# The first block's convolution branch of a fused adaLN, S4 convolution and SwiGLU kernel: row additions on GpSimd and high and low parts in place of fp32 products

## The chip, the cores and the metric

The kernel runs on one core of one Trainium2 chip. A core has five engines that run their own instruction streams: TensorE (PE, matrix products; its weight loads are listed apart as PEld), VectorE (DVE), ScalarE (ACT), GpSimd (POOL) and SyncE (SP, which here only issues DMAs). They hand work to each other by semaphores. Operands lie in SBUF, an on-chip memory of 128 partitions; TensorE writes its sums to PSUM, which VectorE and ScalarE read.

The metric is the time of one execution on the device in microseconds (us), as the median of several runs.

## The reference

`x` is 2048 rows of 448 channels. Six vectors come from a condition `c`; a layer norm scaled and shifted by two of them feeds a long convolution (S4), whose result is added to `x` through a gate; a second such norm feeds a SwiGLU with 1792 hidden channels, added through another gate.

```python
mod = (silu(c) @ w_mod).reshape(c.shape[0], 6, 1, -1)
sa, ca, ga, sb, cb, gb = (mod[:, i] for i in range(6))
h = layernorm(x) * (1 + ca) + sa
x = x + ga * A_ref(h, ...)            # the convolution along the rows
h = layernorm(x) * (1 + cb) + sb
x = x + gb * ((silu(h @ w_gate) * (h @ w_up)) @ w_down)

# A_ref, per channel d:
K[d, l] = real(sum_n C[d, n] * exp(dt[d] * A[d, n] * l) * dt[d] * B[d, n])
y = causal convolution of h with K along l (by FFT) + h * Dskip
```

## The kernel before

**Tiles and blocks.** The 2048 rows are 16 tiles of 128 rows, taken in six blocks (`BLOCKS = [2, 2, 3, 3, 3, 3]`). For each block `ffn` runs the SwiGLU over its tiles, in 14 groups of 128 hidden channels ("column groups", index `f`). `gate_up(f)` makes both projections of group `f` with 22 products into two PSUM banks; `down(f - 1)` stands behind it and adds three products a tile into the banks `DN[q]`. Between them ScalarE makes the silu `p` (L744), VectorE the gated product (L757), ScalarE its high part `phi` (L760) and VectorE its low part `plo` (L761).

**High and low parts.** A product in full fp32 costs TensorE several passes. The kernel splits an operand in a high part of a shorter type (fp32r) and the low rest, and makes three fast products: high by high, high by low, low by high. The weights are split too, and this happens only in block 0 (`fresh`), while they arrive: for each column group ScalarE casts the high parts (L123, L115) and VectorE subtracts the low ones, L125 and L127 for the gate and up weights `gu`, L117 for `wdl` of the down weights. So block 0 has all this work beside that of every block.

**The convolution as running sums.** A test on the decay (`flag`) sets two branches; these inputs take the one for small decay, `small_path`. There the convolution kernel is a straight line in `l`, so the convolution is two cumulative sums along the rows: products of gated parts `v0 = h * gm0` and `v1 = h * g0` with a triangular matrix of ones, `tri`. What the rows of earlier tiles add is carried in two rows of `run` (`run0` and `run1`): each tile leaves its sum in partition 127, a DMA on ScalarE's queue brings it to partition 0, and there it enters the next tile's sum.

**Stages.** While block `b` runs its SwiGLU, the convolution branch of block `b + 1`'s tiles runs beside it in small stages: `s0` makes `h`; `s1` the two gated parts (L908); `s2` adds the running rows to row 0 of the gated parts (L913, L914) and splits `v0` in `vh` (ScalarE, L921) and `vl` (VectorE, L922); `s3` multiplies `h` by `gd` (L927); `s4` makes three products (L933 to L935: `tri` with `vh`, `v1`, `vl`, in this order) and adds `h` to `x`; `s5` makes the next running rows (L957 to L959) and adds the sums to `x`. In block 0 another stage, `s4f`, stands for `s2` to `s4`: it leaves row 0 as it is, multiplies `v0` in full fp32 (L946), and adds the running rows by two fp32 products of one row (L947, L948). After the stages come the statistics of the second norm, the normalised tile `xn` (L193 on VectorE, L194 and L195 on ScalarE) and its transposes (L206), from which ScalarE takes the high part `hhi` and VectorE the low part `hlo`.

**What sets the order.** Each engine runs its instructions in the order in which the program issues them. The table `TIMES` gives it: for each block when the first norm's statistics are taken, its root, a list of half-steps for the stages and the second statistics of each tile, the second root, and the half-steps of `xn`. Half-step `h` means: in column group `h // 2`, right behind `gate_up` where `h` is even, behind `down` where it is odd. In `gate_up(f)` of block 0 the splits of weight group `f + 2` stand between the silu, product, `phi` and `plo` of group `f`. The opening, from the first load to the first product of block 0, follows a list written by hand, `PLAN`, with one word a step; `first_rows` and `gate_0` follow it at the start of block 0's branch.

**PSUM.** Eight banks: four turn round under `bank()`, three are `DN[0]` to `DN[2]`, one is `CV`.

Of the kernel before, what the change touches and what calls it, by code (L numbers as in the profile page):

```python
# [43 lines left out]
m1 k1 cpc gd h11 hd0 ck v01 sq0 o10 v10 w0 cbw o12 v11 w01 o01 o02 hd1 o13 o14 xh1 gc0 sa st0 fs sp gq r0 n10 spc x1 xn0 gc1 st1 sbt tr0  # L44
qtb sbc r1 fl n11 l1 gbk hi00 xn1 w02 tr1 hi01 lo00 hi1 lo01 lo1 d00 d01 w1 w11 gb w12"""
# [11 lines left out]
def tile_kernel(ctx, tc, x, a_re, a_im, b_re, b_im, c_re, c_im, log_dt,  # L57
# [54 lines left out]
    def split_d(j, part=None):  # L112
        hi, lo = wp[j]
        if not part:
            sc.copy(hi, wdn[j])  # L115
        if part != 0:
            ve.tensor_tensor(lo, wdn[j], f32(hi), op=OP.subtract)  # L117
# [16 lines left out]
    run0, run1 = run[:, 0, :], run[:, 1, :]  # L134
    ca1 = const.tile([128, D], F32)
# [133 lines left out]
    with tc.tile_pool(name="pre", bufs=1) as pre:  # L269
# [99 lines left out]
        def turned_to(ps, t):  # L369

            for k in range(4):
# [38 lines left out]
        def to_channels(q):  # L410
            pk[q] = bank()
            turned_to(pk[q], h2[q])
# [7 lines left out]
        def high(q, ks=range(4)):  # L420
            for k in ks:
                c_ = slice(q * 128, (q + 1) * 128)
                sc.activation(hhi[:, k, c_], pk[q][:, k * 128:(k + 1) * 128], AF.Identity, bias=sbc[:, k:k + 1])

        def low(q, ks=range(4)):
            for k in ks:
                c_ = slice(q * 128, (q + 1) * 128)
                ve.scalar_tensor_tensor(hlo[:, k, c_], pk[q][:, k * 128:(k + 1) * 128], sbc[:, k:k + 1], f32(hhi[:, k, c_]),
# [8 lines left out]
        def flag_sum():  # L437
            pe.matmul(psm["d"][0:1, 460:462], ones, sz, start=True, stop=True)

        def flag_of():  # L440
            zm = pre.tile([1, 1], F32)
            ve.tensor_reduce(zm, psm["d"][0:1, 460:462], axis=AX.X, op=OP.add)
# [28 lines left out]
            "qtb": copy(gb, lambda: psm["gq"][:, 0:D]), "gb": copy(gb, lambda: psm["gq"][:, 0:D]),  # L471
# [15 lines left out]
            **{f"xn{q}": (lambda q: lambda: sc.activation(h2[q], h2[q], AF.Copy, scale=n2.of[q][1]))(q) for q in range(2)},  # L487
            **{f"tr{q}": do(to_channels, q) for q in range(2)}, "hi1": do(high, 1),
# [6 lines left out]
            **{f"d0{z}": do(split_d, 0, z) for z in range(2)},  # L495
# [197 lines left out]
    def first_rows():  # L693

        e = slice(96, 128)
        sc.copy(run1[e], CV[e, 0:D])
# [374 lines left out]
```

## Time and profile before

| | us |
|---|---|
| median of 3 runs | 485.05 (484.31 to 485.37) |
| the profiled execution | 485.06 |
| its span from the first instruction to the last | 483.0 |
| TensorE busy | 471.6 |
| VectorE busy | 285.1 |
| ScalarE busy | 155.4 |
| GpSimd busy | 59.8 |

The mean clock that the throttle granted to TensorE was 0.999 of full speed, so no time goes to a lowered clock. Times below are microseconds from the start of the span. A line of the timeline reads: start, duration, engine, source line, operation, result and operands with their shapes, count of like instructions in a row, and in brackets how long the engine had stood idle before it and what it had waited for. A line of a group of instructions reads: source line, engine, operation, operands, count, then busy time in all, mean nanoseconds of one, idle time before them and what ended most of it. In such lines the buffers' numbers are left out, and names are those of the program: `bank`, `dn` and `cv` are PSUM banks, `raw` is a buffer that several things share in turn.

### The profile page before, as it was taken

Reading aid. Unit: us, or ns where it says so; the run is one execution under the profiler, and the core shown is the slowest. Engines: PE = TensorE matmul, PEld = TensorE weight load, DVE = VectorE, ACT = ScalarE, POOL = GpSimd, SP = SyncE. Lnnn points to the kernel's source line nnn. Section 1 sums busy time; section 2 is a strip of 40 time slices with the busy share of each in tenths; the row PEclk is TensorE's granted clock in tenths of the full one; section 3 lists DMA queues with packets and bytes.
Section 4 is the critical chain, followed back from the end, with each engine's and each line's share of the span. In section 5 each row is a group of like instructions: output and inputs, shape, how many; then the busy total and the mean of one; then the engine's idle time right before and its main releaser. Section 6 shows DMA issues by size and latency. Waiting matters only on the chain.

```text
span 483.0 us, 7024 instructions
## 1 busy us (share of the span) xinstructions
PE 471.6 (98%) x2743; PEld 444.9 (92%) x2743; DVE 285.1 (59%) x550; ACT 155.4 (32%) x336; POOL 59.8 (12%) x82
## 2 busy tenths in 40 slices
PE   6999999999999999999999999999999999999995
PEld 4668988999999999999999999999999999999995
DVE  4879998768876546573644757375475544221225
ACT  5876545522234222332312323331222232112111
POOL 1220000000000040310022221002241000000000
PEclk9999999999999999999999999999999999999999
DMA  8965563020001200111200011130001112000001
GB/s 307 405 225 165 194 188 103 0 96 2 1 2 39 58 1 0 45 38 51 92 25 0 2 44 46 43 115 0 2 2 44 45 43 77 22 1 0 1 1 62
DMA packets 18778, 31.24 MB, mean 65 GB/s; under 512 B 2608, under 2 KB 13488, under 8 KB 18736
## 3 DMA queue, kind: packets, MB, share of 16 engines
q1 hardware_dynamic: 18000, 30.52, 18.8%
q8 instruction: 23, 0.38, 0.3%
q10 hardware_dynamic: 736, 0.19, 0.2%
q14 instruction: 19, 0.16, 0.1%
HBM read 24.61 MB, written 6.03 MB: 63 GB/s over the span
## 4 chain that ended last, share of the span: by engine, by line
PE 92%; DMA 3%; DVE 2%; ACT 1%; issue 0%; POOL 0%; SPq 0%; ACTq 0%; DVEq 0%
PE bank L729 59%; PE dn L773 28%; DMA wm<-in_w_mod_groups_dram 2%; DMA x<-in_A_u_dram 1%; PE bank L238 1%; PE dn L449 1%; PE bank L934 1%; PE cv L933 1%; PE cv L935 0%; PE bank L947 0%; DVE x L812 0%; PE bank L206 0%; PE cv L946 0%; PE cv L948 0%; ACT raw L195 0%
## 5 line engine op out<-in xcount | busy, mean ns | idle before, releaser
L729 PE MATMUL bank<-hhi,gu 128*128 128x384 f32 (+1 forms) x1169 | 211.3, 320 | 0.0
L729 PEld LDWEIGHTS bank<-hhi,gu 128*128 128x128 f32 x1169 | 191.2, 188 | 3.1 <-issue 0.7
L729 PE MATMUL bank<-hlo,gu 128*128 128x384 f32 (+1 forms) x668 | 131.8, 319 | 0.0
L757 DVE TENSOR_TENSOR bank<-raw,bank 128x384 f32<-128x384 f32 (+1 forms) x69 | 36.9, 534 | 125.0 <-PE bank L729 121.6
L729 PEld LDWEIGHTS bank<-hlo,gu 128*128 128x128 f32 x668 | 110.2, 188 | 0.0
L760 ACT CAST phi<-bank 128x384 fp32r<-128x384 f32 (+1 forms) x83 | 36.9, 444 | 141.6 <-DVE bank L757 141.6
L744 ACT ACTIVATE raw<-bank 128x384 f32<-128x384 f32 (+1 forms) x70 | 32.9, 470 | 123.0 <-PE bank L729 114.9
L761 DVE TENSOR_TENSOR plo<-bank,phi 128x384 fp32r<-128x384 f32 (+1 forms) x83 | 42.5, 512 | 37.1 <-ACT phi L760 37.1
L773 PE MATMUL dn<-wdh,phi 128*128 128x448 f32 x218 | 58.3, 368 | 0.6 <-DVE run L698 0.4
L773 PE MATMUL dn<-wdh,plo 128*128 128x448 f32 x218 | 57.7, 366 | 0.0
L773 PE MATMUL dn<-wdl,phi 128*128 128x448 f32 x218 | 57.6, 365 | 0.0
L773 PEld LDWEIGHTS dn<-wdl,phi 128*128 128x128 f32 x218 | 41.0, 188 | 3.4
L773 PEld LDWEIGHTS dn<-wdh,plo 128*128 128x128 f32 x218 | 40.9, 188 | 3.3
L773 PEld LDWEIGHTS dn<-wdh,phi 128*128 128x128 f32 x218 | 38.9, 188 | 2.9 <-DVE run L698 0.7
L167 POOL TENSOR_SCALAR rsb<-mvb 128x1 f32<-128x1 f32 (+2 forms) x13 | 4.6, 354 | 171.9 <-DVE mvb L151 171.9
L167 POOL TENSOR_SCALAR rsa<-mva 128x3 f32<-128x3 f32 (+1 forms) x6 | 2.4, 396 | 116.1 <-DVE mva L151 116.1
L123 ACT CAST gu<-raw 128x1024 fp32r<-128x1024 f32 x14 | 14.6, 1046 | 0.0
L125 DVE TENSOR_TENSOR gu<-raw,gu 128x768 fp32r<-128x768 f32 x14 | 13.3, 953 | 0.1
L922 DVE TENSOR_TENSOR vl<-m,vh 128x448 fp32r<-128x448 f32 x12 | 9.1, 757 | 6.7 <-ACT vh L921 6.1
L908 POOL TENSOR_TENSOR m<-m,gm 128x448 f32<-128x448 f32 x9 | 10.4, 1154 | 21.4 <-DVE m L184 17.5
L194 ACT ACTIVATE raw<-raw,rsb 128x64 f32<-128x64 f32 x14 | 4.8, 346 | 21.0 <-DVE raw L193 11.9
L927 POOL TENSOR_TENSOR m<-m,gd 128x448 f32<-128x448 f32 x9 | 11.6, 1284 | 0.0
(232 smaller groups left out, 411.0 us busy)
## 6 DMA issues: line engine op xcount, KB each, us to landing
raw<-in_B_w_gate_up_dram SPq DMA_DIRECT2D x14, 512.0 KB, 3.9
rawd<-in_B_w_down_dram SPq DMA_DIRECT2D x16, 224.0 KB, 4.1
x<-in_A_u_dram SPq DMA_DIRECT2D x12, 224.0 KB, 3.3
out_dram<-x SPq DMA_DIRECT2D x11, 224.0 KB, 2.0
xd<-raw SPq DMA_DIRECT2D x9, 256.0 KB, 2.0
raw<-xd SPq DMA_DIRECT2D x36, 64.0 KB, 2.0
wm<-in_w_mod_groups_dram SPq DMA_DIRECT2D x5, 448.0 KB, 8.2
wm<-in_w_mod_groups_dram SPq DMA_DIRECT2D x5, 336.0 KB, 8.2
```

The lines of the kernel that those rows point to most:

```text
L123: sc.copy(wgu[j][:, :, 0:4, :], w)
L125: en.tensor_tensor(lo, w[:, :, 0:3, :], f32(hi), op=OP.subtract)
L167: po.tensor_scalar(rs[:, 0:n], self.mv[:, 0:n, 1], EPS, None, op0=OP.add)
L729: pe.matmul(ps[s][:, 0:n], w[:, s, a], (hlo if lo else hhi)[:, k, 0:n], start=first and q == 0, stop=end and q == len(ka) - 1)
L744: sc.activation(p[:, 0:n], ps[0][:, 0:n], AF.Silu)
L757: ve.tensor_tensor(ps[1][:, 0:n], p[:, 0:n], ps[1][:, 0:n], op=OP.mult)
L760: sc.copy(hi[:, 0:n], ps[1][:, 0:n])
L761: ve.tensor_tensor(lo[:, 0:n], ps[1][:, 0:n], f32(hi[:, 0:n]), op=OP.subtract)
L773: pe.matmul(dn[q][:, 0:D], u[:, cs], v, start=f == 0 and z == 0, stop=f == (NF - 3 if last else NF - 1) and z == 2)
L908: (ve if on_v else po).tensor_tensor(v, h, g, op=OP.mult)
L922: ve.tensor_tensor(vl, v0, f32(vh), op=OP.subtract)
L927: (ve if on_v else po).tensor_tensor(h, h, gd, op=OP.mult)
```

## The change

Line numbers behind the change are some 3 higher than before for the same code (`gate_up`'s L757 becomes L760, the row additions' L913 and L914 become L916 and L917, the gated parts' L908 becomes L911).

- **Block 0's branch.** `s4f` goes. The stages of block 0 are now `s0`, `s1`, `rows_p`, `s3`, `split`, `s4`, `s5`: the gated parts, both additions of running rows and the product with `gd` are GpSimd's, `split` makes `vh` and `vl`, and `s4` makes its three products, as in the other blocks. Block 0's row of `TIMES` has eight half-steps a tile instead of five, and the first norm's root stands at half-step 3 instead of 5.
- **The opening.** The three copies of `first_rows` become steps of `PLAN` (`fr1`, `fr0`, `fx`), ahead of the branch. The second tile's transposes go to two banks (a `bank()` for channels 0 to 255, `DN[2]` for the rest), its normalisation is shared (256 columns on ScalarE, 192 on VectorE), the copy of `gb` is VectorE's, the cast of the first high part of `w_down` comes earlier on ScalarE, and its low part is GpSimd's. The flag's sum goes to `CV`. In column group 0 the gate takes a `bank()` instead of `DN[2]`.
- **Block 1.** The half-steps of its three normalised tiles go from 23, 24, 24 to 23, 23, 23.

```diff
 TIMES = (
-    ((1, 1), 5, ((5, 10, 15, 15, 15), (9, 9, 18, 19, 19)), 19, (22, 23)),
-    ((2, 3, 3), 3, (...), 23, (23, 24, 24)),
+    ((1, 1), 3, ((5, 6, 8, 9, 11, 12, 13, 13), (9, 10, 15, 12, 17, 18, 19, 19)), 19, (22, 23)),
+    ((2, 3, 3), 3, (...), 23, (23, 23, 23)),
...
+    end = slice(96, 128)
...
         def flag_sum():
-            pe.matmul(psm["d"][0:1, 460:462], ones, sz, start=True, stop=True)
+            pe.matmul(CV[0:1, 460:462], ones, sz, start=True, stop=True)
...
-            "gb": copy(gb, lambda: psm["gq"][:, 0:D]),
+            "gb": lambda: ve.tensor_copy(gb, psm["gq"][:, 0:D]),
...
+            "xn1": lambda: sc.activation(h2[1][:, 0:256], h2[1][:, 0:256], AF.Copy, scale=n2.of[1][1]),
+            "xn1b": lambda: ve.tensor_scalar(h2[1][:, 256:D], h2[1][:, 256:D], n2.of[1][1], None, op0=OP.mult),
+            "fr1": copy(run1[end], CV[end, 0:D]), "fr0": add(run0[end], run1[end], DN[1][end, 0:D]),
+            "fx": copy(xs[0], DN[0][:, 0:D]),
+            "tr0": do(to_channels, 0), "tr1": do(to_channels, 1, (0, 1)), "tr1b": do(to_channels, 1, (2, 3)),
...
-            **{f"d0{z}": do(split_d, 0, z) for z in range(2)},
+            "d00": do(split_d, 0, 0), "d01": do(split_d, 0, 1, po),
...
     def first_rows():
-        e = slice(96, 128)
-        sc.copy(run1[e], CV[e, 0:D])
-        sc.copy(xs[0], DN[0][:, 0:D])
-        ve.tensor_tensor(run0[e], run1[e], DN[1][e, 0:D], op=OP.add)
         sc.dma_start(run[0:1], run[127:128])
...
-                ps = [DN[2] if fresh and f == 0 else bank(), bank()]
+                ps = [bank(), bank()]
...
+        def rows(i, en=ve):
             h, v0, v1 = vs[i]
+            en.tensor_tensor(v0[0:1], v0[0:1], run0[0:1], op=OP.add)
+            en.tensor_tensor(v1[0:1], f32(v1[0:1]), run1[0:1], op=OP.add)
+
+        def rows_p(i):
+            rows(i, po)
...
+        def split(i):
             h, v0, v1 = vs[i]
             vh = work.tile([128, D], F32R, name="vh")
             vl = work.tile([128, D], F32R, name="vl")
...
-        def s4f(i):
-            h, v0, v1 = vs[i]
-            o = CV[:, 0:D]
-            s = bank()[:, 0:D]
-            pe.matmul(s, tri, v1, start=True, stop=False)
-            pe.matmul(o, f32(tri), v0, start=True, stop=False)
-            pe.matmul(s, f32(tri[0:1, :]), run1[0:1], start=False, stop=True)
-            pe.matmul(o, f32(tri[0:1, :]), run0[0:1], start=False, stop=True)
-            s3(i, True)
-            ve.tensor_tensor(xs[i], h, xs[i], op=OP.add)
-            vs[i] = o, s
...
-        return lambda b: ((s0, v(s1), s4f, s5), (s0, v(s1), v(s2), v(s3), s4, s5),
-                          (s0, s1, v(s2), s3, s4, s5))[min(b, 2)]
+        return lambda b: ((s0, s1, rows_p, s3, split, s4, s5), (s0, v(s1), s2, v(s3), s4, s5),
+                          (s0, s1, s2, s3, s4, s5))[min(b, 2)]
```

The order of instructions shows three places. The first is GpSimd in block 0. Before, it stands still between the roots of the first norm (`rsa`) and of the second (`rsb`):

```order
L167 TENSOR_SCALAR rsa_613<-mva_512 128x2
L168 TENSOR_TENSOR rsa_613<-rsa_613,mhalf_107 128x2
L167 TENSOR_SCALAR rsb_984<-mvb_873 128x2
L168 TENSOR_TENSOR rsb_984<-rsb_984,mhalf_107 128x2
L167 TENSOR_SCALAR rsa_1268<-mva_1252 128x3
```

Now the two tiles' five instructions each stand there (`m5` holds two tiles' `h` and two tiles' `v0`; `run` holds the running rows):

```order
L169 TENSOR_TENSOR rsa_568<-rsa_568,mhalf_107 128x2
L911 TENSOR_TENSOR m5_79<-m5_79,gm0_91 128x448
L911 TENSOR_TENSOR v1_661<-m5_79,g0_90 128x448
L916 TENSOR_TENSOR m5_79<-m5_79,run_87 1x448
L917 TENSOR_TENSOR v1_661<-v1_661,run_87 1x448
L936 TENSOR_TENSOR m5_79<-m5_79,gd_94 128x448
L911 TENSOR_TENSOR m5_79<-m5_79,gm0_91 128x448
L911 TENSOR_TENSOR v1_763<-m5_79,g0_90 128x448
L936 TENSOR_TENSOR m5_79<-m5_79,gd_94 128x448
L916 TENSOR_TENSOR m5_79<-m5_79,run_87 1x448
L917 TENSOR_TENSOR v1_763<-v1_763,run_87 1x448
L168 TENSOR_SCALAR rsb_996<-mvb_834 128x2
```

So the second tile's row additions, which need the running rows that the first tile's `s5` leaves, stand behind its product with `gd`, and the second root stands behind all ten.

The second place is VectorE from the last steps of the opening to column group 0 (`gu` are weight groups, `hlo` the low part of the normalised tiles, L757 and L761 product and `plo` of a column group). Before:

```order
L127 TENSOR_TENSOR gu0_146<-raw_80,gu0_146 64x2x128
L428 SCALAR_TENSOR_TENSOR hlo_93<-bank_392,sbc_95,hhi_92 128x128 x4
L428 SCALAR_TENSOR_TENSOR hlo_93<-bank_414,sbc_95,hhi_92 128x128 x4
L117 TENSOR_TENSOR wdl0_151<-rawd0_81,wdh0_150 128x448
L125 TENSOR_TENSOR gu1_148<-raw_80,gu1_148 128x2x384
L127 TENSOR_TENSOR gu1_148<-raw_80,gu1_148 64x2x128
L503 TENSOR_LOAD flag_96
L1002 COMPARE_AND_BRANCH
L757 TENSOR_TENSOR bank_472<-p_469,bank_472 128x256
L125 TENSOR_TENSOR gu2_159<-raw_80,gu2_159 128x2x384
L761 TENSOR_TENSOR plo_471<-bank_472,phi_470 128x256
L127 TENSOR_TENSOR gu2_159<-raw_80,gu2_159 64x2x128
```

And now:

```order
L492 TENSOR_SCALAR h2_1_250<-h2_1_250,rsb_401 128x192
L474 COPY gb_76<-bank_370 128x448
L127 TENSOR_TENSOR gu0_146<-raw_80,gu0_146 64x2x128
L431 SCALAR_TENSOR_TENSOR hlo_93<-bank_393,sbc_95,hhi_92 128x128 x4
L431 SCALAR_TENSOR_TENSOR hlo_93<-bank_415,sbc_95,hhi_92 128x128 x2
L431 SCALAR_TENSOR_TENSOR hlo_93<-dn2_70,sbc_95,hhi_92 128x128 x2
L451 TENSOR_TENSOR run_87<-run_87,dn1_69 32x448
L125 TENSOR_TENSOR gu1_148<-raw_80,gu1_148 128x2x384
L127 TENSOR_TENSOR gu1_148<-raw_80,gu1_148 64x2x128
L511 TENSOR_LOAD flag_96
L998 COMPARE_AND_BRANCH
L760 TENSOR_TENSOR bank_477<-p_473,bank_477 128x256
```

VectorE has two steps more before the first L127 and one less (`wdl0`) behind the low parts; the step for `run` came from behind the branch to before it.

The third place is ScalarE at the end of block 1, where the three normalised tiles (pairs of `L194` and `L195`, now `L195` and `L196`) are made between the silus and casts of the last column groups. Before:

```order
L744 ACTIVATE raw_80<-bank_1673 128x256
L760 CAST phi_1671<-bank_1674 128x256
L194 ACTIVATE raw_80<-raw_80,rsb_1707 128x64
L195 ACTIVATE raw_80<-raw_80,rsb_1707 128x448
L744 ACTIVATE raw_80<-bank_1715 128x256
L760 CAST phi_1713<-bank_1716 128x256
L194 ACTIVATE raw_80<-raw_80,rsb_1707 128x64
L195 ACTIVATE raw_80<-raw_80,rsb_1707 128x448
```

And now the silu of the last group but one stands behind all three pairs:

```order
L747 ACTIVATE raw_80<-bank_1685 128x256
L763 CAST phi_1683<-bank_1686 128x256
L195 ACTIVATE raw_80<-raw_80,rsb_1719 128x64
L196 ACTIVATE raw_80<-raw_80,rsb_1719 128x448
L195 ACTIVATE raw_80<-raw_80,rsb_1719 128x64
L196 ACTIVATE raw_80<-raw_80,rsb_1719 128x448
L195 ACTIVATE raw_80<-raw_80,rsb_1719 128x64
L196 ACTIVATE raw_80<-raw_80,rsb_1719 128x448
L747 ACTIVATE raw_80<-bank_1733 128x256
```

More of the change, by code (lines that the diff above doesn't have):

```diff
@@ L408, in left_over, with to_channels @@
                 pe.matmul(CV[:, 0:D], all1, v1[q], start=q == 0, stop=q == 1)
-        def to_channels(q):
-            pk[q] = bank()
-            turned_to(pk[q], h2[q])
+        def to_channels(q, ks=range(4)):
+            ps = DN[2] if 0 not in ks else bank()
+            for k in ks:
+                pk[q, k] = ps
+            turned_to(ps, h2[q], ks)
         def skip(q):
```

37 lines of the change are left out of this document (17 added, 20 removed), and 2 rows, old and new, of the table TIMES.

## The prediction

> **What bounds the kernel.** I read the page first, then the busy time by stretch, then single rows of the timeline.
>
> ```profile
> span 483.0 us, 7024 instructions
> PE 471.6 (98%) x2743; PEld 444.9 (92%) x2743; DVE 285.1 (59%) x550; ACT 155.4 (32%) x336; POOL 59.8 (12%) x82
> ...
> PE 92%; DMA 3%; DVE 2%; ACT 1%; issue 0%; POOL 0%; SPq 0%; ACTq 0%; DVEq 0%
> ```
>
> TensorE carries 92% of the chain that ended last: work taken from it, or a wait of it, counts fully. The 59% of VectorE is an average; by stretch it reads otherwise.
>
> ```profile
> core 0: us, PE busy (x) PEld busy (x) DVE busy (x) ACT busy (x) POOL busy (x), PEclk, DMA share, GB/s
> 40.00:65.00 25.00, 24.88 (x176) 23.86 (x176) 24.32 (x48) 14.63 (x28) 1.17 (x2) 1.00 0.61 189
> ```
>
> From 40 to 65 us, in block 0, VectorE is busy 24.32 of 25 us, as full as TensorE, because it splits the weights there. ScalarE has 10 us left, GpSimd nearly all. So in block 0 a delay of VectorE of more than a little reaches TensorE. That decides this change.
>
> **Term 1, the products.** The fp32 products and the one-row products of `s4f` go; three products as in block 1 take their place. Weight loads (PEld) before and behind the group, both tiles of block 0, then one of block 1:
>
> ```profile
> 64.06 0.19 PEld L945 LDWEIGHTS bank<-v,tri 128*128 128x128 f32 x1
> 67.00 0.88 PEld L729 LDWEIGHTS bank<-hhi,gu 128*128 128x128 f32 x7 [0.65 <-issue]
> 73.43 0.19 PEld L945 LDWEIGHTS bank<-v,tri 128*128 128x128 f32 x1
> 76.29 0.30 PEld L773 LDWEIGHTS dn<-wdh,phi 128*128 128x128 f32 x2 [0.65 <-ACT run L957]
> 128.78 0.19 PEld L933 LDWEIGHTS cv<-vh,tri 128*128 128x128 f32 x1
> 129.39 0.98 PEld L729 LDWEIGHTS bank<-hhi,gu 128*128 128x128 f32 x7
> ```
>
> The groups took 67.00 - 64.06 = 2.94 and 76.29 - 73.43 = 2.86 us; block 1's takes 129.39 - 128.78 = 0.61. Saved: 2.33 + 2.25 = 4.58. The weight loads behind the first old group ran 0.1 us quicker (0.88 against 0.98), so I take **-4.5**, bounds -4.3 to -4.6.
>
> **Term 2, the start.** `first_rows` moves ahead of the branch, the second tile's transposes go into two banks, its normalisation is shared by ScalarE and VectorE, and the first low part of w_down goes to GpSimd.
>
> ```profile
> 28.25 0.53 ACT L465 COPY qts<-bank 128x448 f32<-128x448 f32 x1 [2.15 <-PE bank L251]
> 39.20 0.19 PEld L773 LDWEIGHTS dn<-wdh,phi 128*128 128x128 f32 x1 [0.37 <-ACT x L697]
> 39.45 0.63 DVE L698 TENSOR_TENSOR run<-run,dn 32x448 f32<-32x448 f32 x1
> 40.10 0.68 DVE L703 SCALAR_TENSOR_TENSOR gm<-g,ntok,gm 128x448 f32<-128x448 f32 x1
> 40.12 0.19 PEld L773 LDWEIGHTS dn<-wdh,phi 128*128 128x128 f32 x1 [0.73 <-DVE run L698]
> 42.83 0.43 DVE L757 TENSOR_TENSOR bank<-p,bank 128x256 f32<-128x256 f32 x1
> 43.29 0.37 ACT L760 CAST phi<-bank 128x256 fp32r<-128x256 f32 x1 [0.74 <-DVE bank L757]
> 43.75 0.31 PEld L773 LDWEIGHTS dn<-wdh,phi 128*128 128x128 f32 x2
> ```
>
> The two waits of the first down product, 0.37 + 0.73 = 1.10, go: what they wait for is done earlier. But the next thing is late at once. The high part phi of column group 1 ends at 43.29 + 0.37 = 43.66, and its reader on TensorE starts at 43.75: no slack. That chain moves only as far as VectorE does. VectorE loses the run step there (40.10 - 39.45 = 0.65), and gets two steps further ahead, the copy of gb and the 192 columns of the second tile; both stand before L127 and the eight low parts and take back part. Bounds: +0.3 (VectorE waits there for GpSimd's new step, see term 4) to -1.2; I take **-0.5**, nearest to the run step's row. The cast of wdh moved ahead lies in ScalarE's 2.15 us of waiting. The flag's sum now holds up `l1`, but the transposes behind `l1` wait for ScalarE anyway; were that cover gone, `l1` could delay them by the two small flag steps. SP's load of weight group 3, queued behind L127, goes out later by as much as L127; its readers come only after groups 1 and 2.
>
> **Term 3, the turn into block 2.** Three normalised tiles in a row instead of one, then a column group's gate, then two:
>
> ```profile
> 143.98 0.35 ACT L194 ACTIVATE raw<-raw,rsb 128x64 f32<-128x64 f32 x1 [1.14 <-DVE raw L193]
> 144.94 0.37 ACT L744 ACTIVATE raw<-bank 128x256 f32<-128x256 f32 x1
> 146.21 0.42 DVE L761 TENSOR_TENSOR plo<-bank,phi 128x256 fp32r<-128x256 f32 x1 [0.44 <-ACT phi L760]
> 148.05 0.14 PEld L206 LDWEIGHTS bank<-ident,raw 128*128 128x128 f32 x1
> 149.30 0.42 PEld L206 LDWEIGHTS bank<-ident,raw 128*128 128x128 f32 x4 [0.80 <-ACT raw L195]
> 150.01 0.36 PEld L206 LDWEIGHTS bank<-ident,raw 128*128 128x128 f32 x3
> 150.34 0.30 PEld L773 LDWEIGHTS dn<-wdh,phi 128*128 128x128 f32 x2
> ```
>
> Three transposes take 150.34 - 150.01 = 0.33, so twelve need 1.3; they took 150.34 - 148.05 = 2.29, so at most 1.0 is to be had. ScalarE's pair takes 144.94 - 143.98 = 0.96, so three end at about 146.9. What is late next is the gate of group 12 behind them: p, product, phi and plo (0.37 + 0.43 + 0.37 + 0.42, with steps of 0.04 between) end at about 148.6, and the second group of transposes needs the bank that plo reads. 149.30 - 148.6 gives **-0.7**, bounds 0 to -1.0.
>
> **Term 4, GpSimd beside VectorE.** Block 0's gated parts, row additions and the product with gd go to GpSimd: ten instructions, five a tile. In exchange the split needs vh (ScalarE, which has room) and vl (VectorE, which loses six steps). Here the trace shows what the new neighbour costs:
>
> ```profile
> L922 DVE TENSOR_TENSOR vl<-m,vh x12: 624/626/1153, 114.5 to 374.8; 128x448 fp32r<-128x448 f32 x12
> ...
> 192.48 0.72 POOL L167 TENSOR_SCALAR rsb<-mvb 128x1 f32<-128x1 f32 x1 [13.70 <-DVE mvb L151]
> ...
> 195.17 1.16 POOL L908 TENSOR_TENSOR v<-m,g 128x448 fp32r<-128x448 f32 x1
> 195.65 1.15 DVE L922 TENSOR_TENSOR vl<-m,vh 128x448 fp32r<-128x448 f32 x1 [1.48 <-ACT vh L921]
> 196.28 1.53 POOL L927 TENSOR_TENSOR m<-m,gd 128x448 f32<-128x448 f32 x1
> 196.73 0.55 DVE L757 TENSOR_TENSOR bank<-raw,bank 128x384 f32<-128x384 f32 x1
> ...
> 206.65 0.23 POOL L167 TENSOR_SCALAR rsb<-mvb 128x1 f32<-128x1 f32 x1 [8.84 <-DVE mvb L151]
> ```
>
> vl takes 0.626 us, but 1.153 when GpSimd is inside an instruction: it ends 0.47 behind GpSimd's (195.17 + 1.16), and GpSimd's next lasts 1.53. L757, which reads PSUM, runs its 0.55 beside it. So a VectorE step with two SBUF inputs waits for GpSimd's instruction to end, here by 0.53. The Trainium skill, "SBUF — State Buffer", section "SBUF: two separate sides", says so: VectorE with two SBUF inputs and GpSimd hold one port pair in turn, for a whole instruction, and the loser fully blocks. It speaks against this change, and the trace agrees (1.153 against 0.626). Without that rule and these rows term 4 would be nothing and the sum 479.4.
>
> Where it bites:
>
> ```profile
> 55.70 0.63 DVE L908 TENSOR_TENSOR m<-m,gm 128x448 f32<-128x448 f32 x1
> 56.78 0.62 DVE L117 TENSOR_TENSOR wdl<-rawd,wdh 128x448 fp32r<-128x448 f32 x1
> 58.97 0.42 DVE L127 TENSOR_TENSOR gu<-raw,gu 64x256 fp32r<-64x256 f32 x1
> 59.08 0.30 PEld L773 LDWEIGHTS dn<-wdh,phi 128*128 128x128 f32 x2
> L125 DVE TENSOR_TENSOR gu<-raw,gu 128x768 fp32r<-128x768 f32 x14 | 13.3, 953 | 0.1
> L913 DVE TENSOR_TENSOR m<-m,run 1x448 f32<-1x448 f32 x12 | 7.2, 604 | 0.0
> L908 POOL TENSOR_TENSOR m<-m,gm 128x448 f32<-128x448 f32 x9 | 10.4, 1154 | 21.4 <-DVE m L184 17.5 <-PE bank L729 3.8
> ```
>
> In times of before: the first tile's vl stands behind L127 of group 7. The two gated parts ahead of it are gone (56.78 - 55.70 = 1.08), so vl would end at 58.97 + 0.42 - 1.08 + 0.63 = 58.94 (0.63 with its start). TensorE needs it for `s4`'s third product, ahead of the down products that begin at 59.08; two products of 0.19 come first: about 59.45. The margin is 0.5. Before vl GpSimd runs five instructions of the first tile and two of the second, with an eighth asking when vl does; a VectorE step with two SBUF inputs (L117, L125, L127, the two steps of h) stands against nearly each. No row of GpSimd on one partition exists; VectorE's one-row step takes 0.604, like its full one, so I take 1.15 for GpSimd's; the lower bound is GpSimd's small step, 0.23. At 0.53 for each of 7.5: 4.0 - 0.5 = 3.5. The second tile's two row additions, with the same margin: 1.05 - 0.5 = 0.5. **+4.0**; bounds 0 (the steps miss each other) and 9.5 x 0.95 - 1.0 = 8.0 (each waits for most of 1.15).
>
> **Sum.** The profiled execution took 485.06 (span 483.0 and 2.06 around it), the median 485.05: no correction. 485.06 - 4.5 - 0.5 - 0.7 + 4.0 = 483.36; I say **483.3**.
>
> **Rivals.** With w the mean wait for a GpSimd instruction, the time is 485.06 - 5.7 + 9.5w - 1.0.
> - The waits hardly reach TensorE, w below 0.35: 479.4 to 481.7. For it: L757 and plo, a third of VectorE's steps, read PSUM and don't wait; GpSimd's instructions may fall on them. Against it: 24.32 of 25 us.
> - On the other side: the wait at the shared access decides, w above 0.80, slower: at 0.95, 487.4. One mechanism: each VectorE step meets GpSimd's instruction near its start, since both ask anew whenever the other ends. For it: GpSimd's small L167 took 0.23 alone but 0.72 where VectorE was busy, so neither goes first by rule and both wait. Against it: the only row of such a wait says 0.53.
> - Between, w from 0.60 to 0.80: 484.1 to 486.0, no change that a measurement could tell (0.2% is about 1 us here).
>
> **Chances.** Forecast (w 0.35 to 0.60, 481.7 to 484.1) 0.38; waits that hardly matter 0.20; no change 0.18; slower 0.24. Faster is thus 0.58. The range must reach into both neighbours: 479.0 to 486.8; the forecast's own is 481.7 to 484.1.
>
> **What would show it.** The three products in block 0 in 0.61 us, if nothing is waited for. In the stretch of column groups 3 to 7, L117, L125 and L127 longer than 0.62, 0.95 and 0.42 beside GpSimd rows, and TensorE idle before the first tile's third product with vl as what ended it: 3.5 us by the forecast, none by the first rival, over 5.5 by the second. At the start, the first down product without its two waits and phi of group 1 still on time's edge. At block 2, transposes with under 0.4 us of waiting. The forecast is wrong if that idle time is far from 3.5, or if it lies elsewhere in block 0.

## The result and the profile after

The changed kernel takes 485.92 us (median of 21 runs, 484.79 to 486.99), the kernel before 485.01 us: a ratio of 1.0018, with a 95% interval of 1.0010 to 1.0026. That is slower by 0.18%, just inside the 0.2% that counts here as no change, and not the 483.3 that was forecast. The profiled execution of the changed kernel took 486.75 us, near the upper end of its runs, so its profile shows more of a loss (span 484.6 against 483.0) than the medians do.

The page of the changed kernel: span, busy time by engine, and the chain that ended last by engine.

```profile
span 484.6 us, 7024 instructions
PE 471.9 (97%) x2735; PEld 446.9 (92%) x2735; DVE 289.9 (60%) x547; ACT 155.5 (32%) x337; POOL 76.4 (16%) x93
...
PE 88%; DVE 6%; DMA 3%; issue 1%; SPq 0%; ACT 0%; POOL 0%; DVEq 0%; POOLq 0%
```

TensorE's share of the chain fell from 92% to 88%, and VectorE's rose from 2% to 6%. VectorE is busy for 4.8 us more than before, although it issues three instructions fewer. The weight loads of TensorE (timeline) show where the terms of the sum went:

```profile
39.65 0.31 PEld L776 LDWEIGHTS dn<-wdh,phi 128*128 128x128 f32 x2
40.78 0.97 PEld L732 LDWEIGHTS bank<-hhi,gu 128*128 128x128 f32 x7
43.82 0.30 PEld L776 LDWEIGHTS dn<-wdh,phi 128*128 128x128 f32 x2 [0.28 <-ACT phi L763]
56.53 0.30 PEld L776 LDWEIGHTS dn<-wdh,plo 128*128 128x128 f32 x2 [0.48 <-DVE plo L764]
60.67 0.19 PEld L942 LDWEIGHTS cv<-vh,tri 128*128 128x128 f32 x1 [1.05 <-ACT vh L930]
64.03 0.29 PEld L944 LDWEIGHTS cv<-vl,tri 128*128 128x128 f32 x1 [3.06 <-DVE vl L931]
64.20 0.71 PEld L776 LDWEIGHTS dn<-wdh,phi 128*128 128x128 f32 x2
78.00 0.19 PEld L942 LDWEIGHTS cv<-vh,tri 128*128 128x128 f32 x1
78.52 0.39 PEld L776 LDWEIGHTS dn<-wdh,phi 128*128 128x128 f32 x2
150.53 0.68 PEld L207 LDWEIGHTS bank<-ident,raw 128*128 128x128 f32 x6
151.83 0.30 PEld L776 LDWEIGHTS dn<-wdh,phi 128*128 128x128 f32 x2
```

The first down product stands without its two waits, and the one of column group 1 now waits 0.28 us for its phi. The second tile's three products take 78.52 - 78.00 = 0.52 us where the old group took 2.86. The transposes into block 2 take 151.83 - 150.53 = 1.30 us instead of 2.29. But TensorE waits up to and in the first tile's products: 0.48 for plo, 1.05 for vh and 3.06 for vl, 4.59 us in all. And behind that the next weight loads take double: 0.71 for two, against 0.39 at 78.52. By stretch of 1 us, with the granted clock as the third column from the right:

```profile
core 0: us, PE busy (x) PEld busy (x) DVE busy (x) ACT busy (x) POOL busy (x), PEclk, DMA share, GB/s
60.00:61.00 1.00, 0.33 (x2) 0.30 (x2) 1.00 (x1) 1.00 (x4) 1.00 (x2) 1.00 0.92 361
61.00:62.00 1.00, 0.34 (x2) 0.00 (x0) 0.97 (x3) 1.00 (x3) 1.00 (x1) 1.00 0.12 45
62.00:63.00 1.00, 0.00 (x0) 0.00 (x0) 0.97 (x2) 0.30 (x1) 0.92 (x2) 0.63 0.00 0
68.00:69.00 1.00, 1.00 (x7) 1.00 (x6) 0.96 (x2) 0.55 (x1) 0.00 (x0) 0.50 0.89 348
69.00:70.00 1.00, 1.00 (x10) 1.00 (x10) 0.93 (x4) 0.68 (x3) 0.00 (x0) 0.95 0.83 310
```

The clock falls to 0.50 within the wait, at about 62.3 us (the microsecond from 62 has 0.63 in the mean), and comes back at about 69.1 (0.95 in that from 69): TensorE works for 5 us at half speed. VectorE is full through all of it. What it does longer shows in the groups of its instructions in block 0 (count, busy time, mean ns of one), where an instruction's time includes, as the rows further down show, what it waits for GpSimd. Two groups of the kernel before (33.5 to 92.5 us):

```profile
L117 DVE TENSOR_TENSOR wdl<-rawd,wdh 128x448 fp32r<-128x448 f32 x14 | 8.7, 620 | 2.2 <-ACT wdh L115 2.0
L127 DVE TENSOR_TENSOR gu<-raw,gu 64x256 fp32r<-64x256 f32 x13 | 5.5, 423 | 0.4
```

Of the changed kernel (33.66 to 94.96 us):

```profile
L125 DVE TENSOR_TENSOR gu<-raw,gu 128x768 fp32r<-128x768 f32 x13 | 14.2, 1095 | 0.1
L117 DVE TENSOR_TENSOR wdl<-rawd,wdh 128x448 fp32r<-128x448 f32 x13 | 9.7, 747 | 2.1 <-ACT wdh L115 2.0
L127 DVE TENSOR_TENSOR gu<-raw,gu 64x256 fp32r<-64x256 f32 x14 | 7.9, 566 | 0.4
L760 DVE TENSOR_TENSOR bank<-p,bank 128x256 f32<-128x256 f32 x14 | 5.9, 422 | 0.6 <-ACT gu L123 0.4
L931 DVE TENSOR_TENSOR vl<-m,vh 128x448 fp32r<-128x448 f32 x2 | 2.1, 1032 | 0.1
```

L125 had 953 ns before. L760, which reads PSUM, did not get longer (422 ns, 425 before). The steps grew by 13 x 0.142 + 13 x 0.127 + 14 x 0.143 + 2 x 0.41 = 6.3 us in all, for GpSimd's ten instructions. Single rows of the timeline show the two beside each other:

```profile
52.51 1.32 POOL L916 TENSOR_TENSOR m<-m,run 1x448 f32<-1x448 f32 x1
53.80 1.52 POOL L917 TENSOR_TENSOR v<-v,run 1x448 fp32r<-1x448 f32 x1
...
52.86 1.46 DVE L117 TENSOR_TENSOR wdl<-rawd,wdh 128x448 fp32r<-128x448 f32 x1
54.25 0.42 DVE L760 TENSOR_TENSOR bank<-p,bank 128x256 f32<-128x256 f32 x1
54.58 1.57 DVE L125 TENSOR_TENSOR gu<-raw,gu 128x768 fp32r<-128x768 f32 x1
```

L117 begins inside the first row addition and ends 0.5 us behind it; L760 runs its 0.42 inside the second; L125 waits until that is done. So there were two suspects: the time that VectorE loses to GpSimd, and the half clock behind the wait. A third, that the products wait for GpSimd's results themselves, does not hold for the first tile:

```profile
55.30 1.85 POOL L936 TENSOR_TENSOR m<-m,gd 128x448 f32<-128x448 f32 x1
59.78 0.37 ACT L763 CAST phi<-bank 128x256 fp32r<-128x256 f32 x1 [3.03 <-DVE bank L760]
60.05 0.57 ACT L930 CAST vh<-m 128x448 fp32r<-128x448 f32 x1
```

GpSimd's last step for that tile ends at 57.15; ScalarE makes vh only at 60.05, right behind a phi for which it had waited on VectorE.

The same view of block 0 as one stretch serves as a measure for all kernels below: from the first weight load of its first `gate_up` to the first down product behind its last transposes. It leaves out the opening, whose end lies between 32.5 and 34.3 us in these profiles. Of the kernel before:

```profile
33.50:92.48 58.98, 58.33 (x402) 53.35 (x402) 52.74 (x102) 33.56 (x66) 2.35 (x4) 1.00 0.44 138
```

Of the changed kernel:

```profile
33.66:94.96 61.30, 57.48 (x394) 54.43 (x395) 56.82 (x101) 33.47 (x65) 17.88 (x14) 0.94 0.43 137
```

The block is 2.32 us longer, and VectorE (the third busy time) is busy for 4.08 us more in it. In these two profiles the opening ends 0.16 us later, and the time from the end of block 0 to the end of the span is 0.9 us shorter.

### The profile page after: what moved, and what is told of

The parts are those of the page before. It is cut to its first block, busy times and chain, and to the rows that moved or that the text cites. A ratio compares the mean times of both kernels' runs of the same rounds, so it can differ in the third digit from the quotient of the medians.

```text
span 484.6 us, 7024 instructions
## 1 busy us (share of the span) xinstructions
PE 471.9 (97%) x2735; PEld 446.9 (92%) x2735; DVE 289.9 (60%) x547; ACT 155.5 (32%) x337; POOL 76.4 (16%) x93
## 3 DMA queue, kind: packets, MB, share of 16 engines
HBM read 24.61 MB, written 6.03 MB: 63 GB/s over the span
## 4 chain that ended last, share of the span: by engine, by line
PE 88%; DVE 6%; DMA 3%; issue 1%; SPq 0%; ACT 0%; POOL 0%; DVEq 0%; POOLq 0%
PE bank L732 56%; PE dn L776 26%; DMA wm<-in_w_mod_groups_dram 2%; DVE gu L125 1%; DVE gu L127 1%; DMA vec<-in_c_log_dt_dram 1%; DVE wdl L117 1%; PE cv L944 1%; PE cv L942 1%; PE bank L239 1%; PE dn L452 1%; PE bank L943 1%; DVE bank L760 0%; DVE hlo L431 0%; SPq L283 0%
## 5 line engine op out<-in xcount | busy, mean ns | idle before, releaser
L760 DVE TENSOR_TENSOR bank<-raw,bank 128x384 f32<-128x384 f32 (+1 forms) x69 | 36.9, 534 | 124.2 <-PE bank L732 121.9
L911 POOL TENSOR_TENSOR m<-m,gm 128x448 f32<-128x448 f32 x11 | 13.2, 1200 | 28.6 <-DVE m L185 28.6
L125 DVE TENSOR_TENSOR gu<-raw,gu 128x768 fp32r<-128x768 f32 x14 | 15.2, 1085 | 0.1
L931 DVE TENSOR_TENSOR vl<-m,vh 128x448 fp32r<-128x448 f32 x14 | 11.1, 795 | 6.8 <-ACT vh L930 6.1
L936 POOL TENSOR_TENSOR m<-m,gd 128x448 f32<-128x448 f32 x11 | 14.6, 1326 | 0.1
L911 POOL TENSOR_TENSOR v<-m,g 128x448 fp32r<-128x448 f32 x11 | 14.1, 1281 | 0.0
```

The lines of the kernel that those rows point to most:

```text
L125: en.tensor_tensor(lo, w[:, :, 0:3, :], f32(hi), op=OP.subtract)
L760: ve.tensor_tensor(ps[1][:, 0:n], p[:, 0:n], ps[1][:, 0:n], op=OP.mult)
L911: (ve if on_v else po).tensor_tensor(v, h, g, op=OP.mult)
L931: ve.tensor_tensor(vl, v0, f32(vh), op=OP.subtract)
L936: (ve if on_v else po).tensor_tensor(h, h, gd, op=OP.mult)
```

## The experiments

The last column is the block's length less VectorE's busy time.

| kernel | median us | ratio to before, 95% | block 0, us | VectorE busy in it, us | the rest of it |
|---|---|---|---|---|---|
| before | 485.01 | | 58.98 | 52.74 | 6.24 |
| changed | 485.92 | 1.0010 to 1.0026 | 61.30 | 56.82 | 4.48 |
| changed, again | 485.98 | 1.0003 to 1.0029 | 61.79 | 56.60 | 5.19 |
| small steps on GpSimd | 479.37 | 0.9862 to 0.9893 | 54.56 | 50.46 | 4.10 |
| steps on VectorE | 484.21 | 0.9975 to 1.0004 | 59.54 | 55.60 | 3.94 |
| steps on VectorE, other order | 486.25 | 1.0008 to 1.0029 | 60.73 | 56.16 | 4.57 |
| products of the first tile later | 490.45 | 1.0089 to 1.0121 | 65.30 | 56.82 | 8.48 |
| filled wait | 487.15 | 1.0035 to 1.0061 | 60.65 | 56.71 | 3.94 |
| before, ten more GpSimd steps | 491.74 | 1.0114 to 1.0153 | 65.69 | 59.66 | 6.03 |
| the same, of one row | 492.08 | 1.0132 to 1.0183 | 64.88 | 59.52 | 5.36 |
| the same (128 rows), filled wait | 491.90 | 1.0122 to 1.0153 | 65.00 | 59.63 | 5.37 |
| old branch of block 0 | 485.04 | 0.9986 to 1.0022 | 58.91 | 53.17 | 5.74 |
| split in the second tile alone | 483.44 | 0.9951 to 0.9974 | 58.21 | 54.08 | 4.13 |
| the same, earlier | 483.93 | 0.9969 to 0.9991 | 58.76 | 54.32 | 4.44 |

**GpSimd's steps made small.** GpSimd's ten instructions stay, but on 8 columns. The kernel thus leaves out most of the gated parts and running rows of block 0, and its vh and vl are made from `h` without them; it serves only to measure time.

```diff
+        c8 = slice(0, 8)
...
+                po.tensor_tensor(v[:, c8], h[:, c8], g[:, c8], op=OP.mult)
...
+            po.tensor_tensor(v0[0:1, c8], v0[0:1, c8], run0[0:1, c8], op=OP.add)
+            po.tensor_tensor(v1[0:1, c8], f32(v1[0:1, c8]), run1[0:1, c8], op=OP.add)
...
+            po.tensor_tensor(h[:, c8], h[:, c8], gd[:, c8], op=OP.mult)
...
+            sc.copy(vh, h)
+            ve.tensor_tensor(vl, h, f32(vh), op=OP.subtract)
+            vs[i] = h, vh, vl, vh
...
-        return lambda b: ((s0, s1, rows_p, s3, split, s4, s5), ...
+        return lambda b: ((s0, s1_8, rows_8, s3_8, split_8, s4, s5), ...
```

> Edit: GpSimd's five instructions a tile in block 0 work on 8 of the 448 columns, so that they take a fraction of their time; left out is thus the computing of the gated parts and running rows in block 0, vh and vl are made from h, and s4's second product reads vh. All instructions of VectorE, ScalarE and TensorE stay. Theory (each of GpSimd's ten full instructions takes about 0.63 us from VectorE, 6.3 us in all, and through it comes the whole loss): L117, L125, L127 back at 0.62, 0.95, 0.42, waits of TensorE in block 0 under 1 us, time 479.3 to 480.5, which is what the prediction's sum gives without its fourth term. Rival (VectorE lacks the time anyway, since the products' 2.3 us a tile had been its cover): waits of 2 us or more stay, time 481 to 482.5.

479.37 us, faster than before by 5.7 us. Block 0 as a stretch, and VectorE's groups in it:

```profile
33.06:87.62 54.56, 54.41 (x396) 52.40 (x395) 50.46 (x101) 33.71 (x66) 6.80 (x14) 1.00 0.47 153
```

```profile
L125 DVE TENSOR_TENSOR gu<-raw,gu 128x768 fp32r<-128x768 f32 x13 | 12.4, 953 | 0.1
L117 DVE TENSOR_TENSOR wdl<-rawd,wdh 128x448 fp32r<-128x448 f32 x13 | 8.0, 619 | 2.1 <-ACT wdh L115 2.0
L127 DVE TENSOR_TENSOR gu<-raw,gu 64x256 fp32r<-64x256 f32 x14 | 5.9, 423 | 0.4
```

The three lines are back at their old durations, TensorE is busy for 54.41 of 54.56 us, and the clock is 1.00. So all else in the change gives in sum what it should, and the length of GpSimd's steps costs 485.92 - 479.37 = 6.55 us, about what VectorE loses beside them (56.82 - 50.46 = 6.36). Since this kernel also frees vh and vl from GpSimd's results, the next two test the loss without any such link.

**The price by itself.** The kernel before with ten more GpSimd instructions that nobody needs, of 128 rows and, with `scr[0:1]`, `h[0:1]` and `gd[0:1]`, of one row:

```diff
             make_h(h, i)
             vs[i] = h
+            if i in TILES[1]:
+                scr = work.tile([128, D], F32R, name="vh")
+                for _ in range(5):
+                    po.tensor_tensor(scr, h, gd, op=OP.mult)
```

> Edit to the kernel before: GpSimd makes five more products of h with gd into a buffer that nothing reads (vh's, unused in block 0) behind s0 of each of the two tiles of block 0's branch, ten instructions of 128x448 in all; nothing waits for them but the buffers' next use. This is the disputed cost by itself. Theory (0.63 us of VectorE for each, and VectorE has about half a microsecond to spare): L117, L125 and L127 longer by 6 us in sum, time longer by 4 to 6 us, 489 to 491. By the prediction's 0.53: 5.3 in sum and up to 4.3 longer. Rival (no cost, the instructions miss each other): 485.

> As e10_extra, but each of the ten extra instructions works on one partition (1x448). Theory (a GpSimd step of one row lasts as long as one of 128 rows and holds VectorE as long): as e10_extra within 1 us. Rival (a short step): under 486.

491.74 and 492.08 us, 6.6 and 6.9 us longer than the 485.17 of before beside them. The ten instructions on GpSimd (groups, 33 to 96 us), first with 128 rows:

```profile
L903 POOL TENSOR_TENSOR vh<-m,gd 128x448 fp32r<-128x448 f32 x10 | 14.8, 1485 | 7.9 <-DVE m L184 7.3
```

then with one:

```profile
L903 POOL TENSOR_TENSOR vh<-m,gd 1x448 fp32r<-1x448 f32 x10 | 14.8, 1480 | 7.9 <-DVE m L184 7.3
```

One row takes as long as 128. VectorE is busy for 6.92 and 6.78 us more in block 0: 0.69 and 0.68 for each instruction, where I had expected 0.63. And the time grows by as much, to just above the 489 to 491 that I had expected: VectorE had not the half microsecond to spare. Where it is full shows when the block is cut at the same place of its work, at 80 us before and at 86.5 with the ten steps:

```profile
33.50:80.00 46.50, 45.85 (x309) 41.15 (x310) 43.88 (x85) 26.80 (x52) 1.17 (x2) 1.00 0.54 170
33.22:86.50 53.28, 49.07 (x309) 43.58 (x310) 50.87 (x86) 26.75 (x52) 16.02 (x12) 0.94 0.46 149
```

Up to there VectorE lacks 2.6 us of being busy throughout before, and 2.4 with the ten steps: what was added went into the time. The other 3.6 us that it stands idle in the block lie behind that place in both kernels.

**The steps on VectorE instead.**

```diff
-        return lambda b: ((s0, s1, rows_p, s3, split, s4, s5), ...
+        return lambda b: ((s0, v(s1), rows, v(s3), split, s4, s5), ...
```

> Edit: the gated parts, row additions and the product with gd of block 0 on VectorE instead of GpSimd, all else as changed. Theory (VectorE loses a wait at the access that it shares with GpSimd for each of GpSimd's instructions): L117, L125 and L127 return to 0.62, 0.95 and 0.42 us; VectorE does seven steps of about 0.63 itself ahead of the first tile's vl, 4.4 us, against 5.0 us of waits, so vl comes 0.6 us earlier at most and the time is 485 to 486: GpSimd saves VectorE nothing. Rival (VectorE is late for another reason, and GpSimd does take work from it): vl comes 4 us later, TensorE waits about 7 us, time 488 to 490.

484.21 us: faster than the changed kernel by 1.7 us and than the 485 to 486 expected, and against before unclear. VectorE makes all ten steps itself and is still busy for 1.2 us less than with GpSimd's help. The waits for vh and vl are 1.02 and 2.21 us. So GpSimd takes no work off VectorE here.

**Order.** Two attempts to take the wait away by order alone. In the first TensorE's three products come later, with the steps on GpSimd; in the second VectorE makes vl earlier, with the steps on VectorE:

```diff
-    ((1, 1), 3, ((5, 6, 8, 9, 11, 12, 13, 13), (9, 10, 15, 12, 17, 18, 19, 19)), 19, (22, 23)),
+    ((1, 1), 3, ((5, 6, 8, 9, 11, 14, 15, 15), (9, 10, 16, 12, 18, 19, 20, 20)), 20, (22, 23)),
...
+    ((1, 1), 3, ((5, 6, 8, 12, 9, 12, 13, 13), (11, 13, 16, 18, 17, 18, 19, 19)), 19, (22, 23)),
```

> Edit: the half-steps of block 0: the first tile's s4, s5 and second statistics at 14, 15, 15 instead of 12, 13, 13, the second tile's row additions, split, s4, s5, statistics at 16, 18, 19, 20, 20 instead of 15, 17, 18, 19, 19, the second root at 20. Theory (TensorE waits because it asks for vl too early, and the loss of VectorE itself is smaller than the wait): the wait for vl goes, a part comes back at the down products of column group 5, whose plo ends at about 61.6 us (1.2 us of waiting), no wait is over 2 us, the clock stays at 1.00, and the time is 481 to 483. Rival (VectorE is behind by 5 us and stays the bound until its work is done, wherever s4 stands): the same 4 us of waiting in smaller pieces at plo and gu, time 483.5 to 485.

> Edit: as e2_vector (the five steps a tile on VectorE), and in another order: the first tile's split at half-step 9 ahead of its product with gd (12) and ahead of the second tile's steps; the second tile's half-steps are 11, 13, 16, 18, 17, 18, 19, 19. VectorE does the same work as in e2_vector, but five steps (3.2 us) fewer ahead of the first tile's vl, and TensorE's waits for vh and vl there were 1.02 and 2.21 us in e2_vector. Theory one (VectorE's work in block 0, some 57 us of the block's 59.5, is the bound, and order only moves the waits): the waits for vl go and 1 to 2 us of them come back at plo, phi or gu later in the block; time 483 to 484. Rival (the wait was one of order): no wait behind it over 0.3 us, clock 1.00, time 481 to 482.

Both expectations missed, with their rivals: 490.45 and 486.25 us. In the first the wait for the first tile's vl goes, and then the second tile's chain is late: its row additions wait for the DMA of the running rows (timeline, GpSimd and TensorE's weight loads).

```profile
74.08 1.12 POOL L916 TENSOR_TENSOR m<-m,run 1x448 f32<-1x448 f32 x1 [9.92 <-DMA run<-run]
...
79.22 0.19 PEld L942 LDWEIGHTS cv<-vh,tri 128*128 128x128 f32 x1 [2.52 <-ACT vh L930]
80.66 0.29 PEld L944 LDWEIGHTS cv<-vl,tri 128*128 128x128 f32 x1 [1.14 <-DVE vl L931]
```

In the second the waits for vh and vl of the first tile are gone as meant, and 3.1 us of waiting stands some 7 us behind, with 1.09 more for a plo at the end of the block:

```profile
66.73 0.90 PEld L732 LDWEIGHTS bank<-hhi,gu 128*128 128x128 f32 x7 [1.33 <-ACT wdh L115]
69.87 0.50 PEld L776 LDWEIGHTS dn<-wdh,phi 128*128 128x128 f32 x2 [1.77 <-ACT phi L763]
```

Neither order made the waits smaller; both moved them and added to them. In the second VectorE does the same work as in the kernel with the steps on VectorE, and the time is 2.0 us longer. That some third order would do better is not excluded by two attempts.

**The clock.** First the changed kernel once more:

> The changed kernel unaltered, on the same chip as the two others. All theories: 485.5 to 486.3; its place in a second execution shows whether the wait for vl (3 us) and the stretch at the granted clock of 0.50 come again: by the theory that the wait lowers the clock they do, with a length that may differ.

485.98 us; the waits in its profile are 0.51, 1.07 and 3.06 us, and the clock is 0.50 from 64 to 68 us. In both profiles the low clock lasts about 6.8 us. Wait and low clock come together again.

Products into an unused bank fill TensorE's wait, once in the changed kernel, once in the kernel with ten more GpSimd steps. They change no work of another engine.

```diff
             pe.matmul(s, tri, v1, start=True, stop=True)
+            if i == TILES[1][0]:
+                for _ in range(14):
+                    pe.matmul(DN[2][:, 0:D], tri, v1, start=True, stop=True)
             pe.matmul(o, tri, vl, start=False, stop=True)
...
+                def filler():
+                    for _ in range(17):
+                        pe.matmul(DN[2][:, 0:D], tri, wp[0][0], start=True, stop=True)
...
+                    go(12, filler)
```

> Edit: 14 more products of tri with v1 into the bank DN[2], which nothing reads before it is written anew, between the second and the third product of the first tile's s4 in block 0; TensorE waits there for vl. Theory (the idle time of 3.06 us also lowers the granted clock to 0.50, and the work behind it runs at half speed for some microseconds): the wait of the third product shrinks to about 0.3 us, vl ends as late as before, the granted clock stays at 1.00 from 60 to 70 us, the mean clock returns to 0.999, and the time falls by 1 to 2.5 us against the changed kernel, to about 484. Rival (the low clock has another cause and fell there by chance): clock still low in that stretch and the time unchanged at 485.9, or longer by what of the 14 products (2.7 us) does not fit in the wait.

> Edit to e10_extra: 17 products of tri with a part of w_down into DN[2], which nothing reads in this block, ahead of the down products of column group 5, where TensorE waited 3.64 us for phi; they change no time of VectorE. Theory (of the 6.6 us that the ten extra instructions cost, some 2.5 are the low clock behind that wait, more than VectorE's own loss of 5.2): the wait is filled, the granted clock stays at 1.00 from 60 to 72 us, and the time is 489 to 490.5 instead of 491.7. Rival (the loss is VectorE's time alone, and the clock hides in it): 491.3 to 492.

By stretch, the kernel with ten more steps, without the filling products and with them:

```profile
64.00:68.00 4.00, 4.00 (x18) 3.76 (x17) 3.94 (x6) 0.53 (x1) 2.12 (x2) 0.50 0.41 114
```

```profile
64.00:68.00 4.00, 3.66 (x26) 3.22 (x26) 3.94 (x5) 1.41 (x3) 2.96 (x2) 1.00 0.20 33
```

The clock stayed at 1.00 there, and so it did from 60 to 72 us in the changed kernel with its wait filled. So the wait is what lowers it. But the time did not fall, as the theory of both expectations had it: 487.15 us against 485.92, and 491.90 against 491.74, which is where the rival of the second had put it. Weight loads of the changed kernel with the filled wait:

```profile
63.28 0.19 PEld L947 LDWEIGHTS cv<-vl,tri 128*128 128x128 f32 x1 [0.30 <-DVE vl L931]
72.32 0.30 PEld L776 LDWEIGHTS dn<-wdh,plo 128*128 128x128 f32 x2 [0.46 <-DVE plo L764]
76.58 0.19 PEld L947 LDWEIGHTS cv<-vl,tri 128*128 128x128 f32 x1 [0.95 <-DVE vl L931]
92.95 0.20 PEld L207 LDWEIGHTS bank<-ident,raw 128*128 128x128 f32 x2 [0.61 <-DVE plo L764]
```

TensorE, at full speed, runs into VectorE again: 0.46 + 0.95 + 0.61 = 2.0 us of new waits for the 2.5 (half of 5.0 us) that the clock had cost. Block 0 is shorter by 0.65 us here and by 0.69 in the other kernel (65.69 to 65.00). So in these profiles half speed behind the wait cost about 0.7 us of block 0; the rest of it lay beside VectorE's work. The two profiles of the unaltered changed kernel differ by 0.49 us there (61.30 and 61.79), so the figure is rough. Outside the block the changed kernel with the filled wait loses what it won: in its profiled execution (486.84 us) the DMA of the running rows in block 1 took 3.9 us where it took 1.7 in the changed kernel, and 1.5 us of waits follow between 137 and 152 us. Whether the 14 products bring that about, and why the median is 1.2 us longer, stays open. One more figure keeps the price of the low clock open: among the 21 runs of the changed kernel the five with a mean clock of 0.990 or 0.991 have a median of 486.75 us, and the nine with 0.995 or 0.996 one of 485.65. Which of the two brings the other is not shown.

**The opening and block 1 alone**, with block 0's branch as before:

```diff
-    ((1, 1), 3, ((5, 6, 8, 9, 11, 12, 13, 13), (9, 10, 15, 12, 17, 18, 19, 19)), 19, (22, 23)),
+    ((1, 1), 5, ((5, 10, 15, 15, 15), (9, 9, 18, 19, 19)), 19, (22, 23)),
...
-        return lambda b: ((s0, s1, rows_p, s3, split, s4, s5), ...
+        return lambda b: ((s0, v(s1), s4f, s5), ...
```

> Edit: the changed kernel with block 0's branch as before (s4f, its four stages and half-steps): what is left of the change is the opening and block 1's normalised tiles. Theory: -0.7 at the turn into block 2 and -0.3 to -0.5 at the start, no wait for vl and no low clock: 483.8 to 484.2. Rival (the opening costs as much as it saves): 484.3 to 484.5.

485.04 us, with an interval from 0.14% faster to 0.22% slower: above the expectation and its rival, and the 1.2 us that the start and the turn were to give together lies outside the interval, which ends at 0.7 us faster. By themselves the start and the turn are not shown to gain. In its profile, taken at 483.90 us, the transposes into block 2 wait 0.34 us for a silu, where in the changed kernel they do not wait.

**A version that beats both.** Before, VectorE stood idle for 3.1 of the 10 us behind 80 us. So the first tile keeps the old stages, and only the second tile is split, on VectorE and later:

```diff
+    ((1, 1), 5, ((5, 10, 15, 15, 15, 15, 15, 15), (9, 10, 17, 19, 18, 20, 21, 21)), 21, (22, 23)),
...
+        def second(g, other=None):
+            def stage(i):
+                if i != TILES[1][0]:
+                    g(i)
+                elif other:
+                    other(i)
+            return stage
...
+        return lambda b: ((s0, v(s1), second(rows), second(v(s3)), second(split), second(s4, s4f), s5), ...
```

> Edit: the changed kernel's opening and block 1; in block 0 the first tile goes by the stages of before (gated parts and gd on VectorE, s4f with the fp32 and one-row products), the second by rows, split and s4 with all its steps on VectorE, later: half-steps 9, 10, 17, 19, 18, 20, 21, 21, the second root at 21. Theory (VectorE's time bounds block 0 until about 80 us, and behind that it stood idle for 3.1 of 10 us before): the second tile's three more steps of VectorE (1.9 us) fall into that slack, its products save 2.25, the opening 0.4 and block 1 0.7: 485.0 - 3.3 = 481.7, up to 482.5 with small waits. Rival (VectorE has no slack there either): 483.5 to 484.5.

And the second tile a half-step earlier:

```diff
-    ((1, 1), 5, ((5, 10, 15, 15, 15, 15, 15, 15), (9, 10, 17, 19, 18, 20, 21, 21)), 21, (22, 23)),
+    ((1, 1), 5, ((5, 10, 15, 15, 15, 15, 15, 15), (9, 10, 16, 18, 17, 19, 20, 20)), 20, (22, 23)),
```

> Edit to e9_second: the second tile's half-steps are 9, 10, 16, 18, 17, 19, 20, 20 instead of 9, 10, 17, 19, 18, 20, 21, 21, the second root at 20. In e9_second TensorE waited 1.38 us for a plo at the end of block 0, behind the late steps of the second tile. Theory (VectorE's late work there is what is left to win): that wait shrinks by half a microsecond to one, no new wait over 0.5, time 482.5 to 483.2. Rival (VectorE has no free time earlier either): the wait comes back at the second tile's vl, time 483.4 to 484.

The first: 483.44 us, ratio 0.9962 (0.9951 to 0.9974) to before: faster than both kernels, though less than expected and nearly at its rival's 483.5. In its profile, an execution of 482.40 us, the longest wait left stands at the end of block 0, where a plo comes late:

```profile
90.08 0.20 PEld L207 LDWEIGHTS bank<-ident,raw 128*128 128x128 f32 x2 [1.38 <-DVE plo L764]
```

Taking the second tile's steps earlier left that wait at 1.38 us and added 0.5 us to another one there (a silu's): 483.93 us, the expected gain did not come.

## Why the prediction was wrong, point by point

**Products, start, turn: right in sum.** Their sum was -5.7 us. With GpSimd's steps made small the kernel is 5.7 us faster, and block 0 alone is 58.98 - 54.56 = 4.4 us shorter, close to the 4.5 of the products. The turn gave 1.0 in the profile of the changed kernel, the upper bound, instead of 0.7. The start cannot be read from one profile: the two waits of 1.10 us are gone, phi of group 1 became late at once, by 0.28 us, and the end of the opening varies by more than the 0.5 forecast (32.5 to 34.3 us with the new opening, 33.2 to 34.0 with the old). And the kernel with these two terms alone was not faster than before, so how the sum divides stays open.

**GpSimd beside VectorE: right in kind, too small.** Term 4 was +4.0 and is +6.55. Two steps of it failed. The first is the price: 0.53 for each of GpSimd's instructions came from the only row of such a wait; measured are 0.64 in the changed kernel (6.36 / 10) and 0.69 by itself. The second is the margin of 0.5 us a tile. It was the slack of one reader, vl, and taking it off treated the loss as paid once TensorE had waited there. In truth all ten instructions count in full: 6.36 us of VectorE cost 6.55 of time in the changed kernel, 6.92 cost 6.6 in the kernel before. The prediction saw VectorE at 24.32 of 25 us and still counted the loss by a margin instead of adding up VectorE's work for the whole stretch in which it is full, up to about 80 us. That TensorE was as full there, once the products had gone, is seen in the small steps' 54.41 of 54.56 us.

**The sign that it named nearly held, and misleads.** The forecast was to be wrong if TensorE's idle time ahead of the first tile's third product was far from 3.5 us. It was 3.06 for vl, or 4.59 with plo and vh. Up to vl the sum fits with a higher price: vl (L931 of the first tile) ran from 62.54 to 63.98, 5.0 us behind the 58.94 forecast for it without loss, or 0.67 for each of 7.5 instructions. The 0.5 forecast for the second tile did not show: its products did not wait. Against the kernel with small steps, block 0 is 6.74 us longer, of which 3.67 are TensorE's idle time (3.82 against 0.15) and 3.07 its longer busy time (57.48 against 54.41), mostly the half clock. Read from TensorE alone, the waits were forecast about right and the low clock is what was left out. The filled waits show why that reading misleads: with the clock at 1.00 most of those 3 us come back as waits for VectorE.

**The one-row step** was taken to be as long as a full one: right, 1480 against 1485 ns.

**The rivals.** The time fell where the third rival put it (484.1 to 486.0), and its condition, a wait of 0.60 to 0.80, holds with 0.64. That the time lies in its range is partly luck: its formula gives 484.4 for 0.64, and the margin of 1.0 that it takes off is most of what is missing. The first rival (steps that miss each other) is refuted by the groups. The second (a mean wait over 0.80) did not come.

**What no case had** is the granted clock of 0.50 behind the wait. The Trainium skill, "TensorE: Matmul & The Clock Gate", Part 1 (The HAM clock gate), says that a window of about 3.4 us without work halves the clock, and one of sustained work restores it. The trace agrees on the half (0.50); but TensorE was not idle for a whole window here, it had been busy for 0.33 and 0.34 us in the two microseconds ahead of the fall. A wait of 3.5 us was forecast, and with it this should have been a rival. Its price would have been overrated, though: 5.0 us of work at half speed make 2.5 us, and filling the waits shortened block 0 by about 0.7.

**The rule on the shared access** ("SBUF — State Buffer" in the Trainium skill, section "SBUF: two separate sides") agrees with the runs here, one-row instructions included (0.68 us of VectorE for each).

## What to carry to other kernels

Where one stretch keeps two engines equally full, a gain on the one is worth only what the other can follow: add up both engines' work up to the place where one of them stands idle again, with what each loses to a third, and do not count a delay by the slack of its first reader. Moving SBUF-to-SBUF steps from a full VectorE to an idle GpSimd gave nothing here: each took 0.64 to 0.69 us of VectorE, no less than the same steps take on VectorE itself (0.60 to 0.63). A low clock behind a wait is a sign of the wait, and not always a cost of its own: fill the wait to find out.

## What was not expected of the hardware

A GpSimd product of one partition and 448 columns held VectorE as long as one of 128 partitions (0.68 against 0.69 us each), while one of 8 columns held it for nothing that shows (L125 at 953 ns). And the granted clock halved, for 6.8 us, some 1.3 us into the second of two waits (1.05 and 3.06 us, with two products between); in the second profile of the same kernel it fell 2.3 us into that wait and stayed low as long.
